# Decay gates of two batches built in one chain and applied on half-height tiles, and a first FFN tile that turns wide

## The chip, the cores and the metric

The kernel runs on one core of a Trainium2 chip. The core has TensorE (PE in the profile, with its weight loads shown apart as PEld), VectorE (DVE), ScalarE (ACT), GpSimd (POOL) and SyncE (SP, which here only issues DMA transfers). The metric is the device time of one execution in microseconds (us), lower is better; a kernel is run several times and the median is given. The profile is one further execution.

## The reference

Causal attention with a forgetting decay over 8 batches of 8 heads, 576 positions, head dimension 64, then a SwiGLU block on the 4608 tokens:

```python
scores = (q @ k.T) / sqrt(64)
cum    = cumsum(log(clip(f, 1e-4, 1)))           # per batch and head
scores = where(causal, -1e9, scores + cum[:, None] - cum[None, :])
attn   = softmax(scores);  x = attn @ v           # x: 4608 tokens x 512
g      = x @ w_gate                               # 512 x 1536
out    = (g * sigmoid(g) * (x @ w_val)) @ w_out   # 1536 x 512
```

## The kernel before

**Order of the work.** The program builds a list of operations, each with an engine (or a choice of engines), a cost, its predecessors, its buffers and a key, and a planner (class `Plan`, L34) plays them through once: at each moment the ready operation with the lowest key goes next on its engine. The order that comes out is fixed for each engine, and every engine works through its own list in order; at run time it waits where a predecessor is late. So a cost, a key or a `ready` time changes only the order. DMA transfers are played in the plan as rings of SP, ACT and POOL that share the bandwidth by `packet`.

**Stages.** Batch 0 is loaded as q and k "quads" by POOL's DMA (`ld_quad`, L472), turned on TensorE (`turn_two`, L477) and copied ("straightened") by ACT or DVE into `QK` (L485, copies at L303 and L305). Its scores come from `score2` (L629): for head pair jj (heads jj and jj+4, on partitions 0 to 63 and 64 to 127) and bank i (a set of key-tile and query-range segments, `BANKS`, L188) first the q.k products of both heads, 64 rows each (L641), then the gate products that add the decay. `expo` (L656, ACT) takes the exponential, `mask` (L660, POOL) blanks the upper triangle, `weigh` (L671, PE) multiplies by V, `invert` and `scale` (DVE) normalise, `flip` (PE) turns the result and `put` copies it to `xT`. Batch 0 goes in two parts: bank 0 of all four pairs, keys from 0 on, then banks 1 to 3 of the four pairs, keys from 1000 on (`attention2`, L749). Batch 1 is turned the same way (`turn`, `straighten`, key S1_KEY = 1150), but its gates, and those of all later batches, are four extra rows of `QK` that SP loads from the DRAM tensor `dec_d` (`rows`, L521), so that `score` (L618) needs one product of 68 rows. Batches 2 to 7 come through DRAM and a transposing DMA (`narrow`, `turned`), from the planned time PACE0 = 61 on.

**Gates of batch 0** (`gates`, L378). The 32 rows of f of batches 0 to 3 are loaded four times, into the four quarters of the partitions. Then, in two parts of 256 and 320 columns: clip (DVE, L324), Ln (ACT, L327), running sum (DVE, L331); from the sum, in bf16, `hi` (-8 cum, its first quarter apart as `hi0`), `mid` and `low` rests (DVE, L342 to L352), and `up` (8 cum, ACT, L336). `KG` holds the key side of the 32 rows over all 128 partitions, `QG` the query side. For a head the right rows are picked by a column of zeros and ones, `chosen` or `three`, which are summed from the identity (L434 to L436): for bank 0 the product takes that column itself, broadcast (L652), and one more product with a column of the identity brings the query side (L653); for banks 1 to 3 DVE has made a copy of `QG` per head with other rows zeroed (`choose`, L372, eight copies of 320 columns) and one product is enough (L650). All of these use 128 rows.

**Gates of later batches.** The 32 rows of batches 4 to 7 (`lf1`) are clipped on DVE early and go through scan, `later` (L360) and four stores on SP from the planned time 36 on, with the low priority key 9000 (DEC1_KEY). `out0` are the four stores of batches 0 to 3.

**FFN.** The tokens go in tiles of 512; per tile 12 column blocks fc: four products with w_gate and four with w_val (L826), tanh on ACT (L830), two DVE operations (L834, L837), then the output products (L841). The first 512 tokens are two tiles of 256, interleaved by block (`share`), and fill PE's gaps in the early stage. The weights come through POOL's DMA in three and four pieces (`weights`, L816). While PE has nothing in the plan, products on the identity run (L930).

The line that is repeated for every segment of a gate product, for bank 0 and for the others:

```python
nc.tensor.matmul(s[:m, c : c + w], keys, row, start=False, stop=end)                       # L650
nc.tensor.matmul(s[:m, c : c + w], keys, three[:, h : h + 1].to_broadcast([P, w]), ...)    # L652
nc.tensor.matmul(s[:m, c : c + w], ident[:, GR + h : GR + h + 1].to_broadcast([P, m]), QG[:, q0 : q0 + w], ...)  # L653
```

Of the kernel before, what the change touches and what calls it, by code (L numbers as in the profile page):

```python
# [9 lines left out]
F32 = mybir.dt.float32  # L10
# [13 lines left out]
class Op:  # L24
    def __init__(self, eng, fn, after, behind, take, use, key, ready, dma):
# [5 lines left out]
        self.start = self.done = None  # L31


class Plan:  # L34
# [32 lines left out]
    def run(self, idle=None):  # L67
# [30 lines left out]
        while left:  # L98
# [4 lines left out]
            while events and events[0][0] <= t + 1e-9:  # L103
                _, _, kind, o = heapq.heappop(events)
                if kind in ("queue", "dma"):
# [10 lines left out]
                    if kind == "queue":  # L116
                        rings[o.ran].append([o.dma, o])
# [82 lines left out]
PACE = 8.8  # L200
PACE_A = 8.8
PACE0 = 61.0
# [4 lines left out]
def kernel(ctx, tc, q, k, v, f, w_gate, w_val, w_out, out):  # L207
# [46 lines left out]
    three = sb("three", [P, H], BF16)  # L254
    chosen = sb("chosen", [P, H], F32)
# [9 lines left out]
    lf1, cum1, rest = [QK[:GR, i, w, : 2 * S].bitcast(F32) for i, w in ((7, 0), (7, 1), (6, 0))]  # L265
    late = [QK[:GR, i, w, n * S : (n + 1) * S] for i, w, n in ((6, 1, 0), (6, 1, 1), (7, 0, 0), (7, 0, 1))]
    ones = OT[0].bitcast(BF16)[:BH, :S]
    KG, QG = xT[:, 0, S : 2 * S], xT[:, 1, S : 2 * S]
    REST = S - HALF
    G0 = {h: xT[:, 3, 2 * S + HALF * n : 2 * S + HALF * (n + 1)] for n, h in enumerate(h for h in range(H) if h % 4 not in ONEHOT)}  # L270
    G1 = [xT[:, n // 3, 2 * S + REST * (n % 3) : 2 * S + REST * (n % 3 + 1)] for n in range(H)]
# [47 lines left out]
    def ld_f(e, half, n):  # L319
        E[e].dma_start(out=lf1 if half else lf[GR * n : GR * (n + 1)],  # L320
                       in_=f.rearrange("b h s -> (b h) s")[GR * half : GR * (half + 1)])

    def clip(e, lf, c):
        E[e].tensor_scalar(out=lf[:, c], in0=lf[:, c], scalar1=1e-4, scalar2=1.0, op0=ALU.max, op1=ALU.min)  # L324
# [10 lines left out]
    def up(e, c):  # L335
        nc.scalar.activation(QG[GR : 2 * GR, c], cum[GR : 2 * GR, c], AF.Copy, scale=8.0)  # L336

    def hi(e, r, c):
        if e == "ACT":
            nc.scalar.activation(KG[r, c], cum[r, c], AF.Copy, scale=-8.0)  # L340
        else:
            nc.vector.tensor_scalar_mul(KG[r, c], cum[r, c], -8.0)  # L342

    def rest1(e, c):
        nc.vector.scalar_tensor_tensor(
            out=r1[64:, c], in0=cum[64:, c], scalar=-8.0, in1=KG[64:, c], op0=ALU.mult, op1=ALU.subtract)

    def mid(e, c):
        nc.vector.tensor_copy(KG[64:, c], r1[64:, c])

    def low(e, c):
        nc.vector.tensor_sub(KG[96:, c], r1[96:, c], KG[96:, c])  # L352

    def dec_out(e, half, n):
        g = slice(GR * half, GR * (half + 1))
        dst = dec_dram[0, 0, g] if n == 0 else dec_dram[n, 1, g]
        src = late[n] if half else QG[GR : 2 * GR] if n == 0 else KG[(0, 64, 96)[n - 1] :][:GR]
        nc.sync.dma_start(out=dst, in_=src)
# [13 lines left out]
    def choose(e, h, part):  # L372
        if part:
            nc.vector.tensor_scalar_mul(G1[h], QG[:, HALF:], chosen[:, h : h + 1])
        else:
            nc.vector.tensor_scalar_mul(G0[h], QG[:, :HALF], chosen[:, h : h + 1])

    def gates(parts, key):  # L378

        lds = [op(("ACT" if n % 2 else "SP", 0.5), ld_f, 0, n, key=-40, dma=0.3, packet=100) for n in range(4)]  # L380
        ld1 = op(("SP", 0.5), ld_f, 1, 0, key=-39, dma=0.3, packet=100)
        done, s = [], None
        lns = []
        for i, c in enumerate(parts):
            w = c.stop - c.start
            a = op(("DVE", 0.1 + w / 960), clip, lf, c, after=lds, key=key - 1 + 0.1 * i, tag="clip")
            lns.append(op(("ACT", 0.15 + w / 1100), ln, lf, c, after=[a], key=key + 0.1 * i, tag="ln"))
# [465 lines left out]
    def ffn(t, t0, n, hs, lo, share):  # L853
# [3 lines left out]
        for fc in range(KF):  # L857
# [5 lines left out]
            if fc == KF - 1:  # L863
                lg = a
# [131 lines left out]
```

## Time and profile before

| | |
|---|---|
| median of 3 runs | 388.75 us (388.27 to 389.16) |
| profiled execution | 388.2 us, its span 386.5 us |
| PE busy in the first 10.4 us | 6.33 us, most of it products on the identity |
| first score product | starts at 10.43 us |
| gate products L650, L652, L653 | 40, 16 and 16 |
| straightens of batch 1, 64x640 and 64x512 | 8 on ACT (771 and 732 ns), 8 on DVE (816 and 716 ns) |
| POOL transfers, issue to landing | quads 9.2 us, V 8.8 us, w_gate and w_val 12.2 us (medians) |

The span is the time from the first to the last instruction. An engine counts as busy while an instruction is in it; products are pipelined and their ends are modelled, so a PE shown as fully busy is not always at its peak, and the distance from the start of one product to the start of the next says more. The chain of waits follows the work that ended last back from its end: at each step to what released it, or to the instruction before it on its engine; asked for a stretch, it starts at the end of that stretch.

### The profile page before, as it was taken

What the parts mean: (1) busy time and instruction counts of PE and PEld (TensorE: products, weight loads), DVE (VectorE), ACT (ScalarE), POOL (GpSimd) and SP (SyncE); (2) the same over time, 40 slices, a digit from 0 to 9 for tenths busy, and PEclk for the clock granted to TensorE, in tenths of its full rate; (3) what the DMA queues carried; (4) which work ended last, traced back from release to release, by engine and by line L of the source; (5) the groups of instructions that cost most, each with busy time, mean ns of one, the idle gap of its engine ahead of it and who ended that gap; (6) DMA issues with size and microseconds to landing.
All of it is one profiled execution on the core that took longest, in us unless ns stands there. A gap on an engine that the chain in (4) does not pass through costs nothing.

```text
span 386.5 us, 8511 instructions
## 1 busy us (share of the span) xinstructions
PE 375.8 (97%) x3185; PEld 216.1 (56%) x3185; DVE 219.5 (57%) x460; ACT 213.8 (55%) x440; POOL 140.1 (36%) x368
## 2 busy tenths in 40 slices
PE   6997999999999999999999999999999999999996
PEld 4666789545556555555555555555564444444444
DVE  8957988257624773277515772477427725733750
ACT  5978884246756565755666457566673323323322
POOL 8794658005534624444355236522330000000000
PEclk9999999999999999999999999999999999999999
DMA  8999998769679994999699999995131011002003
GB/s 165 194 193 195 206 194 133 170 168 171 124 171 204 154 194 94 210 223 180 128 182 199 197 138 213 231 151 85 46 90 46 0 54 57 0 28 83 0 2 109
DMA packets 125065, 52.01 MB, mean 135 GB/s; under 512 B 111840, under 2 KB 119392, under 8 KB 124256
## 3 DMA queue, kind: packets, MB, share of 16 engines
q1 hardware_dynamic: 108640, 36.18, 46.9%
q0 software_dynamic: 16288, 15.14, 26.9%
q8 instruction: 25, 0.41, 0.4%
q10 hardware_dynamic: 96, 0.15, 0.1%
q14 instruction: 16, 0.13, 0.1%
HBM read 38.63 MB, written 17.11 MB: 144 GB/s over the span
## 4 chain that ended last, share of the span: by engine, by line
PE 94%; DVE 2%; ACT 2%; issue 1%; POOL 0%; DVEq 0%; POOLq 0%
PE ps L826 47%; PE ps L841 24%; PE ps L623 9%; PE ps L681 7%; PE ps L650 2%; ACT QK L303 1%; PE ps L641 1%; PE ps L930 1%; PE ps L698 1%; DVE QK L305 1%; PE ps L652 0%; DVE hh L837 0%; PE ps L482 0%; PE ps L498 0%; PE ps L653 0%
## 5 line engine op out<-in xcount | busy, mean ns | idle before, releaser
L826 PE MATMUL ps<-xT,wg 128*128 128x512 bf16 (+1 forms) x480 | 113.0, 357 | 1.1 <-DVE QK L305 1.0
L830 ACT ACTIVATE th<-ps 128x512 f32<-128x512 f32 (+1 forms) x120 | 66.5, 554 | 86.0 <-PE ps L826 83.6
L826 PE MATMUL ps<-xT,wv 128*128 128x512 bf16 (+1 forms) x480 | 113.0, 357 | 0.5 <-DMA wg<-in_moe_w_gate_dram 0.5
L834 DVE SCALAR_TENSOR_TENSOR th<-th,ps 128x512 f32<-128x512 f32 (+1 forms) x120 | 75.6, 630 | 64.9 <-ACT th L830 64.6
L658 ACT ACTIVATE PT<-ps 128x512 bf16<-128x512 f32 (+2 forms) x192 | 92.6, 508 | 27.6 <-PE ps L623 15.8
L841 PE MATMUL ps<-wo,hh 128*128 128x512 bf16 (+2 forms) x456 | 104.5, 367 | 0.0
L837 DVE TENSOR_TENSOR hh<-th,ps 128x512 bf16<-128x512 f32 (+1 forms) x120 | 76.0, 634 | 13.6 <-PE ps L826 1.8
L667 POOL TENSOR_SCALAR_AFFINE_SELECT PT<-PT 128x128 bf16<-128x128 bf16 (+1 forms) x192 | 52.9, 282 | 71.9 <-ACT PT L658 67.2
L826 PEld LDWEIGHTS <-wg 128*128 128x128 bf16 x480 | 45.5, 97 | 41.2 <-issue 1.4
L826 PEld LDWEIGHTS <-wv 128*128 128x128 bf16 x480 | 45.4, 97 | 37.5 <-issue 0.4
L623 PE MATMUL ps<-QK 68*128 68x256 bf16 x392 | 64.8, 261 | 0.0
L841 PEld LDWEIGHTS <-hh 128*128 128x128 bf16 x456 | 41.8, 97 | 37.1
L667 POOL TENSOR_SCALAR_AFFINE_SELECT PTa<-PTa 128x256 bf16<-128x256 bf16 x64 | 26.2, 412 | 76.1 <-ACT PTa L658 74.9
L688 DVE RECIPROCAL rc<-ps 128x5 f32<-128x5 f32 (+2 forms) x68 | 12.9, 190 | 65.5 <-PE ps L681 65.1
L681 PE MATMUL ps<-VB,PT 128*128 128x65 bf16 x768 | 44.2, 193 | 0.8 <-ACT QK L303 0.8
L681 PEld LDWEIGHTS <-PT 128*128 128x128 bf16 x768 | 37.0, 97 | 13.0 <-issue 1.0
L845 ACT ACTIVATE ot<-ps 128x512 f32<-128x512 f32 (+2 forms) x38 | 21.9, 575 | 39.9 <-PE ps L841 38.2
L623 PEld LDWEIGHTS <-QK 68*128 68x128 bf16 x392 | 31.1, 97 | 13.7
L658 ACT ACTIVATE PTa<-ps 128x384 bf16<-128x384 f32 x64 | 30.9, 488 | 10.3 <-PE ps L623 9.5
L693 DVE TENSOR_TENSOR xn<-ps,rc 128x320 bf16<-128x320 f32 (+2 forms) x72 | 32.3, 453 | 2.2
L681 PEld LDWEIGHTS <-PTa 128*128 128x128 bf16 x192 | 13.7, 98 | 11.3
L305 POOL CAST VB<-natv 128x512 bf16<-128x512 f32 (+1 forms) x32 | 19.0, 613 | 0.2 <-DMA natv<-in_v_dram 0.2
(69 smaller groups left out, 158.6 us busy)
## 6 DMA issues: line engine op xcount, KB each, us to landing
out_dram<-ot SPq DMA_DIRECT2D x35, 256.0 KB
natv<-in_v_dram SPq DMA_DIRECT2D x25, 256.0 KB
qk_d<-in_q_dram POOLq DMA_DIRECT2D x24, 144.0 KB, 3.6
qk_d<-in_k_dram POOLq DMA_DIRECT2D x24, 144.0 KB, 4.3
wg<-in_moe_w_gate_dram POOLq DMA_DIRECT2D x3, 512.0 KB, 11.1
wv<-in_moe_w_val_dram POOLq DMA_DIRECT2D x3, 512.0 KB, 12.4
wo<-in_moe_w_out_dram POOLq DMA_DIRECT2D x4, 384.0 KB, 11.9
xT<-in_q_dram POOLq DMA_DIRECT2D x4, 288.0 KB, 8.7
```

The lines of the kernel that those rows point to most:

```text
L305: E[e].tensor_copy(dst, src)
L623: nc.tensor.matmul(s[:, c : c + w], QK[:KR, hqk[p].i, 1, j * S + kt * P : j * S + (kt + 1) * P], QK[:KR, hqk[p].i, 0, j * S + q0 : j * S + ...
L658: nc.scalar.activation(place(h, i)[:, OFFS[i] : OFFS[i] + c], ps(bs)[:, :c], AF.Exp, scale=0.125)
L667: nc.gpsimd.affine_select(out=d, in_=d, pattern=pat, compare_op=ALU.is_ge, fill=0.0, base=0, channel_multiplier=-1,)
L681: nc.tensor.matmul(o[:, lo : lo + D + 1], pt[:, c : c + P], VB[hvb[b].i][:, kt, hb, : D + 1], start=first and n == 0, stop=last and n == l ...
L693: nc.vector.tensor_mul(XN[bx.i][:, qb : qb + nq, j], o, r)
L826: nc.tensor.matmul(ps(bf)[:, :n], w[:, ko, fc * P : (fc + 1) * P], xT[:, ko, t0 : t0 + n], start=(ko == 0), stop=(ko == KD - 1))
L830: nc.scalar.activation(TH[bt.i][:, :n], ps(bf)[:, :n], AF.Tanh, scale=0.5)
L834: nc.vector.scalar_tensor_tensor(out=t, in0=t, scalar=1.0, in1=ps(bf)[:, :n], op0=ALU.add, op1=ALU.mult)
L837: nc.vector.tensor_mul(HH[bh.i][:, lo : lo + n], TH[bt.i][:, :n], ps(bf)[:, :n])
L841: nc.tensor.matmul(ps(bf)[:m, c], HH[hs[fc].i][:, lo : lo + m], wo[:, fc, c], start=(fc == 0), stop=(fc == KF - 1))
L845: nc.scalar.activation(OT[bo.i][:m, c], ps(bf)[:m, c], AF.Copy, scale=0.5)
```

## The change

- **One gate chain for batches 0 and 1.** 16 rows of f (batches 0 and 1) are loaded four times into partitions 0 to 63, and the clip writes them to both halves (two clips per part). The chain runs on all 128 partitions: `hi`, `less`, `mid`, `less`, `low`, where columns of coefficients (`ct`, made of the identity by reductions) let each group of 16 rows end as its own term. `KG` then holds, in each half, four groups of the 16 rows of batches 0 and 1; 64 further columns are set to zero, so that all key tiles are 128 wide.
- **Gate products on 64 rows.** In `score2` the products of heads jj and jj+4 use the rows of their own half, into two banks, as the q.k products do. For banks 1 to 3 there is one copy `QG[jj]` for both heads (four copies of 320 columns, on ACT or DVE); for bank 0 a column `one` and a column of the identity, and `QS` (8 cum).
- **Later gates.** `lf1` now holds all 64 rows; its clip goes to POOL, its scan and `later` get key 1000 and the planned time 12, its stores (48 rows, batches 2 to 7) the planned time 46. `out0` stores the 8 rows of batch 1. `put` of batch 1 no longer comes after the later stores.
- **Exp table.** The first use of Exp (`o_warm`) comes after the three Ln instead of after the first `up`.
- **FFN.** The first tile is one tile of 512 tokens; its blocks 0 to 3 are done in halves of 256, its blocks 4 to 11 whole.
- **Plan.** S1_KEY 1150 becomes 1350 (batch 1's turns come after batch 0's last scores), PACE0 61 becomes 59, costs of some transfers change, and transfers of SP and ACT that enter after 3.5 us while POOL's ring holds small packets are planned 2.5 us later, once.

```diff
-                        rings[o.ran].append([o.dma, o])
+                        if o.ran != "POOL" and t > 3.5 and not o.late and any(r[1].packet < 900 for r in rings["POOL"]):
+                            o.late = True
+                            push(t + LATE, "queue", o)
+                        else:
+                            rings[o.ran].append([o.dma, o])
...
+    KG = xT[:, 3, S : 2 * S]
+    QG = [xT[:, r, n : n + S] for r, n in ((0, S), (1, S), (2, S), (3, 2 * S + D))]
+    KG_ALL = xT[:, 3, S : 2 * S + D]
+    QS = xT[:, 3, 3 * S + D : 3 * S + D + HALF]
...
+    def less(e, n, c):
+
+        nc.vector.scalar_tensor_tensor(out=r1[:, c], in0=KG[:, c], scalar=ct[:, 4 + n : 5 + n], in1=r1[:, c] if n else cum[:, c],
+                                       op0=ALU.mult, op1=ALU.add)
+
+    def mid(e, c):
+        nc.vector.tensor_scalar_mul(KG[:, c], r1[:, c], -8.0)
+
+    def low(e, c):
+        nc.vector.tensor_scalar(out=KG[:, c], in0=r1[:, c], scalar1=ct[:, 7:8], scalar2=ct[:, 8:9], op0=ALU.mult, op1=ALU.add)
...
+            a = [op(("DVE", 0.1 + w / 960), clip, lf[r], c, lf[:D], after=lds, key=key - 1 + 0.1 * i + 0.01 * n, tag="clip")
+                 for n, r in enumerate((slice(D, P), slice(0, D)))]
+            lns.append(op(("ACT", 0.15 + w / 1100), ln, lf, c, after=a, key=key + 0.1 * i, tag="ln"))
...
+            a = op(("DVE", 0.05 + w * 0.0011), hi, c, after=[s], key=kk, tag="hi")
+            a = op(("DVE", 0.05 + w * 0.0015), less, 0, c, after=[a, o_ct], key=kk)
+            a = op(("DVE", 0.05 + w * 0.0011), mid, c, after=[a], key=kk)
+            a = op(("DVE", 0.05 + w * 0.0015), less, 1, c, after=[a], key=kk)
+            a = op(("DVE", 0.05 + w * 0.0011), low, c, after=[a], key=kk, tag="low")
+            u = op(("ACT", 0.15 + w / 1100), up, c, after=[s], key=kk, tag="up") if i == 0 and ONEHOT else None
...
+        l1 = op(("ACT", 0.67), ln, lf1, slice(0, S), after=[a], key=key + 0.3, tag="ln1")
+        a = op(("DVE", 1.4), scan, cum1, lf1, slice(0, S), after=[l1], key=DEC1_KEY, ready=DEC1_AT, tag="scan1")
...
+    o_warm = op(("ACT", 1.4), lambda e: nc.scalar.activation(warm, warm, AF.Exp), after=lns, key=WARM_KEY)
...
-                keys = KG[:, kt * P : kt * P + m]
+                r, end = slice(D * u, D * (u + 1)), n == len(segs) - 1
+                o, keys = ps(bs[u])[:, c : c + w], KG_ALL[r, kt * P : (kt + 1) * P]
                 if i or jj not in ONEHOT:
-                    row = G1[h][:, q0 - HALF : q0 - HALF + w] if i else G0[h][:, q0 : q0 + w]
-                    nc.tensor.matmul(s[:m, c : c + w], keys, row, start=False, stop=end)
+                    nc.tensor.matmul(o, keys, QG[jj][r, q0 : q0 + w], start=False, stop=end)
                 else:
-                    nc.tensor.matmul(s[:m, c : c + w], keys, three[:, h : h + 1].to_broadcast([P, w]), start=False, stop=False)
-                    nc.tensor.matmul(s[:m, c : c + w], ident[:, GR + h : GR + h + 1].to_broadcast([P, m]),
-                                     QG[:, q0 : q0 + w], start=False, stop=end)
+                    mine = D * u + 6 * H + FB * u + jj
+                    nc.tensor.matmul(o, keys, one[r, jj : jj + 1].to_broadcast([D, w]), start=False, stop=False)
+                    nc.tensor.matmul(o, ident[r, mine : mine + 1].to_broadcast([D, P]), QS[r, q0 : q0 + w], start=False, stop=end)
...
+            parts = [(0, HALF), (HALF, n - HALF)] if t == 0 and fc < WIDE else [(0, n)]
...
-S1_KEY = 1150
+S1_KEY = 1350
-CLIP1 = ('DVE', 0.43)
+CLIP1 = ('POOL', 2.1)
-DEC1_KEY = 9000
-DEC1_AT = 36
+DEC1_KEY = 1000
+DEC1_AT = 12
+DECOUT_AT = 46
+WIDE = 4
```

203 lines of the change are left out of this document (91 added, 112 removed).

## The prediction

> **What bounds the kernel now.** I read the busy times by stage first, then the chain of waits of three early stretches, then the groups of single lines. The whole span first: time, engine, then busy microseconds.
>
> ```profile
> span 386.5 us, 8511 instructions
> PE 375.8 (97%) x3185; PEld 216.1 (56%) x3185; DVE 219.5 (57%) x460; ACT 213.8 (55%) x440; POOL 140.1 (36%) x368
> ```
>
> PE is the bound of the whole, so the end moves only by PE work that disappears or by PE gaps that close. The stages say where gaps are (stretch, its length, then busy us and count of each engine, clock, DMA share, GB/s):
>
> ```profile
> 10.40:14.00 3.60, 3.55 (x100) 2.77 (x100) 3.40 (x10) 3.15 (x7) 2.39 (x5) 1.00 2.25 161
> 14.00:30.00 16.00, 16.00 (x238) 10.90 (x235) 10.39 (x39) 13.08 (x30) 14.59 (x37) 1.00 1.38 198
> 30.00:38.00 8.00, 5.33 (x95) 4.47 (x96) 5.84 (x12) 7.24 (x14) 3.12 (x7) 1.00 1.44 197
> 38.00:50.00 12.00, 11.55 (x117) 9.57 (x117) 11.06 (x27) 10.47 (x27) 8.94 (x21) 1.00 1.21 204
> 50.00:68.00 18.00, 18.00 (x241) 16.11 (x240) 15.32 (x44) 11.35 (x29) 11.76 (x30) 1.00 0.95 162
> ```
>
> From 50 on PE has no gap until the last store; 30 to 38 has 2.67 us of gaps, 38 to 50 has 0.45. Everything that the change touches lies before 68, so the question is how much PE time it takes out of 10.4 to 50. The chain of 10 to 18 shows what PE does there (start, us, what):
>
> ```profile
> 14.89 0.27 PE ps L641 x4
> 15.16 0.21 PE ps L652
> 15.38 0.11 PE ps L653
> 15.49 0.11 PE ps L652
> 15.60 0.11 PE ps L653
> ...
> 16.97 0.27 PE ps L641 x4
> 17.24 0.56 PE ps L650 x4
> 17.79 0.18 PE ps L681 x6
> ```
>
> The reader sees q.k products (L641, 64 rows each) and gate products (L650, L652, L653, 128 rows each). The four L641 stream 256, 256, 128 and 128 columns. At the pace of L652/L653 (a new 256-column product every 0.11 us) they would take 0.32 us one after another, but the next begins after 0.27: the two heads, on different halves of the rows, run side by side, 0.16, and then there is a gap of 0.11. The gates are not side by side: one per 0.11. In 30 to 38 the chain is another:
>
> ```profile
> 30.72 0.78 ACT QK L303
> 32.42 0.83 DVE QK L305
> 33.27 0.78 ACT QK L303
> 35.70 0.77 ACT QK L303
> 36.49 0.74 ACT QK L303
> 37.26 0.73 DVE QK L305
> ...
> 41.85 1.27 DVE QK L331
> 43.15 0.56 DVE QK L364
> 44.56 0.66 DVE QK L366
> ```
>
> There the copies of batch 1's turned q and k on ACT and DVE, and then the late gate chain on DVE, end the waits.
>
> **The change, part by part.** The sum is made against the profiled execution, 388.2 us (span 386.5 and 1.7 around it); the median of the runs shown is 388.75, so 0.55 is added at the end.
>
> Gate products. For each of four head pairs, bank 0 now has eight 128-row products (four of 256, four of 128 columns: 4 x 0.107 + 4 x 0.053 = 0.64 us); they become eight 64-row ones, two at a time: 0.32. Banks 1, 2 and 3 have 2 x (192+320), 2 x (64+320) and 2 x 320 columns at 0.417 ns: 0.43, 0.32, 0.27; halved, 0.51 saved. Per pair 0.83, in all **-3.3**. If the pairs did not overlap it would be 0, if they overlap as L641 does it is all of it; I take all, since L641 is the same shape on the same rows.
>
> Gaps between the two shapes. After each of the 16 L641 groups 0.11 us pass before the gate products; with both on 64 rows this may vanish: 0 to -1.7. I take half, **-0.8**, as a gap is still due wherever a 128-row product (L681) comes next. The Trainium skill ("TensorEngine Tiling (Array Packing)", Key Properties) states that a change of tiling mode drains TensorE. By that rule all 1.7 would go and the sum would be 0.9 lower; the trace's gap of 0.11 agrees with a drain, but which neighbours remain is not shown, so the sum keeps half.
>
> Start. Before the first score at 10.43 the chain holds the Exp table load (8.35, 1.28 us) and its first use (0.20) between two straightens on ACT. The key side was turned by 9.07 (L482), so at best the score comes 0.7 earlier once the load is moved ahead. Against that: the load now waits for all three Ln, the last of them for a clip on POOL; DVE loses the two memsets (0.60) and the sums L434 to L436 (0.45), gains about ten small ones of 0.12 to 0.17 (1.2 to 1.7) behind the identity, two more clips of about 0.3 to 0.4, and a chain of 5 instead of 4 (256 columns: 0.29+0.42+0.29+0.42+0.29 = 1.71 against 1.42). The memsets left before 4.4 cover about 1 us of it. Range -0.7 to +1.0, I take **-0.2**.
>
> POOL's clip. The 576-column clip leaves DVE (0.91, L324) and goes to POOL behind the fourth quad load, at 4.9. No row shows it on POOL: the cast of 512 columns takes 0.613 (0.69 at 576), the 256-column mask 0.41, which at 576 and twice for two operations is 1.85. I take 1.85, the masks being nearer to an ALU operation. Queued behind it on POOL are five loads of V (0.84 each), two weight loads, and then the masks. POOL had 1.2 us idle before the first mask at 12.02 and 0.8 at 15.1, so most is covered; without that cover it is 1.85 on the first mask. Behind ACT's Ln for it stand the table load and straightens. **+0.3**, range 0 to 1.85.
>
> DVE and ACT. Gone: eight picks (8 x 0.419 = 3.4 on DVE), `up` and `hi0` of the second part and `hi0` of the first (0.47+0.47+0.42 on ACT). New: four picks on DVE or ACT (0.32 to 0.47). Moved: the late chain (1.34+0.56+0.74+0.50+0.74 = 3.9 on DVE, 0.67 on ACT) from 41.8 to somewhere after 12. DVE has 5.6 us idle in 14 to 30, which hides it; where it stood, PE had only 0.42 us of waits: **-0.4**, range 0 to -0.5. Its four stores stay at about 46 on SP, with batch 2's V loads behind them as before (49.24). The loads of f shrink from five of 72 KB to four of half and one of double that; the four stores of batch 1's rows stay.
>
> First FFN tile. Of 12 column blocks, 8 go from two halves to one: 128 products of 256 columns (0.110 each, 14.1 us) become 64 of 512 (0.216, 13.8): **-0.3**. ACT saves 8 x (2 x 0.38 - 0.55), DVE 16 x (2 x 0.41 - 0.63), about 1.7 and 3.0 us, both under a PE without gaps from 50 on: 0. Wide blocks need all 512 tokens of batch 0; four narrow ones (4 x 1.76 = 7 us of PE) stand ahead of them, and the turns of batch 1 now come after the scores, so the second half is ready sooner. Batch 2's release, planned 2 us earlier (59 for 61), falls where PE has no gap: 0.
>
> What comes back. PE saves 4.1 us inside 10.4 to 30, but ACT is busy 16.2 of 19.6 there; with -0.94 for the second `up` and `hi0`, +0.94 for half the picks and +0.67, its slack is 2.7. ACT waits for PE in that stretch for some 2.4 us (1.5 on L650, 0.6 on L653, 0.3 on flips). Only that can close, so 1.7 must come back as new PE gaps, all 4.1 if nothing closes. FFN blocks could fill a part, but each 256-wide one costs ACT 0.38 and DVE 0.83. I take **+2.0**, range 0 (later gaps fill) to 4.1.
>
> Sum: -3.3 - 0.8 - 0.2 + 0.3 - 0.4 - 0.3 + 2.0 = -2.7: 385.5 for the profiled execution, **386.0** as a median. Own range of this case 384.3 to 387.6. A difference of 0.2%, 0.8 us, is about what a measurement tells here.
>
> **Rivals.** *ACT and DVE take it all back*: the stretch to 38 is theirs already (7.24 of 8 us on ACT, copies in the chain), PE only waits longer. For it: these rows, and ACT's total early work hardly changes. Against: in 14 to 30 the chain is PE alone. Price: 4.1 come back instead of 2.0: 388.1. The Trainium skill ("TensorEngine Tiling (Array Packing)", PSUM Bottleneck) says just this: tiling speeds TensorE, not the emptying of PSUM. The trace bears it out in 30 to 38, not in 14 to 30.
>
> *Everything counts*: the saved time stays, the drain gaps go, and the 2.67 us of gaps in 30 to 38 are filled, since copies of batch 1 come when FFN work is at hand. Without the 2.0 and with 0.9 more of gaps: -5.6, 383.1. Against it: the copies still need 12 us of ACT and DVE.
>
> *Slower: POOL's queue sets the first 50 us.* POOL is busy 13.4 of 14 us in 16 to 30, and everything loaded by it is moved by the clip's 1.85. If landing, not PE, ends the waits (first weigh on V, copies on the quads, FFN on weights), the PE saving is idle time and the delay is paid: +1.85 - 0.3 and 0.5 for ACT's Ln in order: +2.1, 390.8. It decides as soon as the queue's delay exceeds its backlog. For it: L474 waited 0.8 on a V load, L826 0.5 on a weight load. Against: loads land 9 to 12 us after issue, so issue is ahead of transfer.
>
> *The pairs do not overlap*: no 3.3, no gaps saved, nothing to come back: -0.6, 388.15. L641 speaks against it.
>
> **How the numbers follow.** Forecast 0.47; everything counts 0.15; taken back 0.12; no overlap 0.04; POOL's queue 0.22. Faster: the first two and a little of the next, 0.64; same 0.14; slower 0.22. The range goes from 383.0 (the best case) to 390.8 (POOL's case), leaving out the outer halves of these, 0.18.
>
> **What would show it.** Gate products of two heads in pairs 0.11 us apart for 256 columns: the first step. No 0.11 gap after L641: the second. First score before 10.4 and the table load before the first straighten: the start. ACT above 90% in 14 to 30 with PE gaps that ACT ends: what comes back. POOL idle before its first mask: the clip covered; a first weigh that waits for DMA, or PE gaps above 4 us in 10 to 40, would make the prediction wrong, and so would batch 0's last weigh later than 33.4.

## The result, and the profile after

The changed kernel takes 387.87 us (median of 9 runs, 387.40 to 388.35), the kernel before 389.16 beside it (9 runs, 388.27 to 389.94): 0.9968 of the time before, 95% interval 0.9957 to 0.9979, so 1.24 us less. In two further rounds of runs (chips 9 and 5) the ratio was 0.9960 [0.9946, 0.9973] and 0.9956 [0.9939, 0.9972]. The forecast was 2.75 less (386.0 for 388.75): the direction held, less than half of the size came. The profiled execution took 387.93. The first lines of its page: span, busy time of each engine, and the granted TensorE clock in 40 slices of 9.65 us:

```profile
span 386.2 us, 8313 instructions
...
PE 372.8 (97%) x3082; PEld 208.8 (54%) x3129; DVE 218.3 (57%) x445; ACT 212.9 (55%) x433; POOL 142.6 (37%) x369
...
PEclk9699999999999999999999999999999999999999
```

PE is busy 3.0 us less than before (372.8 for 375.8), but the span is only 0.3 shorter. The second slice of the clock row has a 6. The stages that the prediction showed, now in the changed kernel, in the same columns (stretch, length, then busy us and count of PE, PEld, DVE, ACT, POOL, then clock, DMA share, GB/s):

```profile
10.40:14.00 3.60, 3.08 (x61) 2.43 (x62) 3.46 (x7) 3.08 (x7) 3.60 (x6) 0.52 2.16 166
14.00:30.00 16.00, 15.38 (x256) 9.95 (x256) 12.83 (x39) 13.46 (x32) 15.23 (x33) 0.89 1.46 189
30.00:38.00 8.00, 6.87 (x126) 5.28 (x125) 7.14 (x16) 7.02 (x14) 5.24 (x15) 1.00 1.39 199
38.00:50.00 12.00, 11.66 (x103) 8.76 (x102) 8.02 (x19) 10.50 (x26) 6.39 (x18) 1.00 1.22 196
50.00:68.00 18.00, 17.83 (x192) 11.12 (x193) 13.60 (x28) 11.31 (x24) 10.35 (x29) 1.00 0.86 154
```

PE's gaps from 10.4 to 38 were 2.72 us and are 2.27; the clock, 1.00 there before, is 0.52 in the first stage and 0.89 in the second. In steps of 2 us:

```profile
8.00:10.00 2.00, 1.06 (x40) 0.76 (x39) 1.82 (x8) 1.64 (x4) 1.94 (x3) 1.00 1.20 231
10.00:12.00 2.00, 1.21 (x40) 0.98 (x40) 2.00 (x4) 1.48 (x3) 2.00 (x3) 0.64 1.68 188
12.00:14.00 2.00, 2.00 (x25) 1.45 (x22) 1.86 (x5) 2.00 (x5) 2.00 (x4) 0.50 2.45 154
14.00:16.00 2.00, 2.00 (x42) 1.30 (x41) 1.06 (x3) 0.95 (x3) 1.71 (x3) 0.50 2.04 174
16.00:18.00 2.00, 2.00 (x25) 1.06 (x23) 2.00 (x6) 1.76 (x5) 1.52 (x3) 0.65 1.24 206
```

PE runs at half speed for 1.44 + 2 + 2 + 1.40 = 6.8 us (if the clock is either full or half, 0.64 is half speed for 1.44 of 2 us, and so on), after a stretch in which it was busy only about half of the time. "PE busy 2.00" does not tell half speed from full. The half that is lost is 3.4 us of PE work, in the very stage where the side-by-side products save theirs. The products themselves (the timeline; start, duration):

```profile
17.50 0.34 PE L658 MATMUL ps<-QK 64*128 64x256 bf16 x4
17.68 0.27 PE L669 MATMUL ps<-one,xT 64*128 64x256 bf16 x2
17.79 0.27 PE L670 MATMUL ps<-xT,ident 64*128 64x256 bf16 x2
17.90 0.22 PE L669 MATMUL ps<-one,xT 64*128 64x128 bf16 x2
17.95 0.22 PE L670 MATMUL ps<-xT,ident 64*128 64x128 bf16 x2
```

Each line of L669 and L670 is a pair, one product per head: 0.11 us for two of 256 columns, 0.05 for two of 128, and from the q.k products (L658) to the first gate product 0.18 with 0.16 of columns: no gap of 0.11. The Trainium skill ("TensorEngine Tiling (Array Packing)", Key Properties) says that TensorE drains when the tiling mode changes; the rows agree, since 64 rows follow 64 rows here without the gap.

The start came later. The chain of waits up to the first score product:

```profile
3.50 7.38 DMA xT<-in_q_dram
10.88 0.04 issue
10.93 0.99 PE ps L499 x21
11.91 0.43 PE ps L658 x4
```

The third quad lands at 10.88, its turn (L499) stands ahead of the first score in PE's order, and the first score starts at 11.84 (before 10.43). The quads take 5.4 to 8.1 us from issue to landing, before 4.4 to 7.4: the two stores of ones on SP now start at 2.73 instead of 3.49, beside them. In two further traces of the changed kernel the first score starts at 11.43 and 11.75.

**One measure for all runs.** The first output product (`wo`, L857) starts at 67.75 in the kernel before and at 67.63 after, and from there to the end 318.75 and 318.6 us pass; in 15 of the 18 runs below it is 318.6, in e4, g1 and g3 318.3 to 318.8. So a difference in span is made before that product, and for those 15 its start tells it to about 0.1 us in one traced execution.

### The profile page after: what moved, and what is told of

It is laid out like the page before. It is cut to its first block, busy times and chain, and to the rows that moved or that the text cites. A ratio compares the mean times of both kernels' runs of the same rounds, so it can differ in the third digit from the quotient of the medians.

```text
span 386.2 us, 8313 instructions
## 1 busy us (share of the span) xinstructions
PE 372.8 (97%) x3082; PEld 208.8 (54%) x3129; DVE 218.3 (57%) x445; ACT 212.9 (55%) x433; POOL 142.6 (37%) x369
## 3 DMA queue, kind: packets, MB, share of 16 engines
q0 software_dynamic: 16288, 15.14, 26.1%
## 4 chain that ended last, share of the span: by engine, by line
PE 92%; DVE 2%; DMA 2%; ACT 1%; issue 1%; POOL 1%; ACTq 0%; POOLq 0%
PE ps L842 48%; PE ps L857 24%; PE ps L640 10%; PE ps L697 7%; DMA xT<-in_q_dram 2%; PE ps L658 1%; ACT QK L309 1%; DVE QK L311 1%; PE ps L714 1%; DVE xn L709 1%; PE ps L944 1%; PE ps L499 0%; ACT PT L674 0%; POOL xT L491 0%; PE ps L666 0%
## 5 line engine op out<-in xcount | busy, mean ns | idle before, releaser
L846 ACT ACTIVATE th<-ps 128x512 f32<-128x512 f32 (+1 forms) x112 | 65.3, 583 | 84.2 <-PE ps L842 82.8
L842 PE MATMUL ps<-xT,wg 128*128 128x512 bf16 (+1 forms) x434 | 109.8, 371 | 0.8
L842 PE MATMUL ps<-xT,wv 128*128 128x512 bf16 (+1 forms) x432 | 109.7, 371 | 0.9
L850 DVE SCALAR_TENSOR_TENSOR th<-th,ps 128x512 f32<-128x512 f32 (+1 forms) x112 | 74.6, 666 | 63.2 <-ACT th L846 63.0
L857 PE MATMUL ps<-wo,hh 128*128 128x512 bf16 (+2 forms) x439 | 101.5, 367 | 0.9
L853 DVE TENSOR_TENSOR hh<-th,ps 128x512 bf16<-128x512 f32 (+1 forms) x112 | 74.8, 669 | 12.3 <-PE ps L842 0.8
L842 PEld LDWEIGHTS <-wg 128*128 128x128 bf16 x448 | 42.5, 97 | 41.2 <-issue 0.2
L640 PE MATMUL ps<-QK 68*128 68x256 bf16 x392 | 63.8, 260 | 0.1
L842 PEld LDWEIGHTS <-wv 128*128 128x128 bf16 x448 | 42.2, 97 | 38.7
L857 PEld LDWEIGHTS <-hh 128*128 128x128 bf16 x456 | 42.2, 97 | 37.8
L697 PE MATMUL ps<-VB,PT 128*128 128x65 bf16 x768 | 43.1, 193 | 0.8 <-issue 0.7
L709 DVE TENSOR_TENSOR xn<-ps,rc 128x320 bf16<-128x320 f32 (+2 forms) x72 | 32.3, 453 | 2.2
L697 PEld LDWEIGHTS <-PTa 128*128 128x128 bf16 x192 | 13.7, 98 | 12.6 <-POOL PTa L683 1.1
L311 POOL CAST VB<-natv 128x512 bf16<-128x512 f32 (+1 forms) x32 | 19.1, 616 | 0.0
## 6 DMA issues: line engine op xcount, KB each, us to landing
wg<-in_moe_w_gate_dram POOLq DMA_DIRECT2D x3, 512.0 KB, 10.4
```

The source lines that it names most:

```text
L311: E[e].tensor_copy(dst, src)
L640: nc.tensor.matmul(s[:, c : c + w], QK[:KR, hqk[p].i, 1, j * S + kt * P : j * S + (kt + 1) * P], QK[:KR, hqk[p].i, 0, j * S + q0 : j * S + ...
L697: nc.tensor.matmul(o[:, lo : lo + D + 1], pt[:, c : c + P], VB[hvb[b].i][:, kt, hb, : D + 1], start=first and n == 0, stop=last and n == l ...
L709: nc.vector.tensor_mul(XN[bx.i][:, qb : qb + nq, j], o, r)
L842: nc.tensor.matmul(ps(bf)[:, :n], w[:, ko, fc * P : (fc + 1) * P], xT[:, ko, t0 : t0 + n], start=(ko == 0), stop=(ko == KD - 1))
L846: nc.scalar.activation(TH[bt.i][:, :n], ps(bf)[:, :n], AF.Tanh, scale=0.5)
```

## The experiments

"Ratio" is against the kernel before on the same chip; "first output" is the start of the first output product in the traced execution, "clock" the mean granted clock of that execution.

| kernel | median us | ratio, 95% interval | span | first score | first output | clock |
|---|---|---|---|---|---|---|
| before | 389.16 | 1 | 386.5 | 10.43 | 67.75 | 0.999 |
| changed | 387.87 | 0.9968 [0.9957, 0.9979] | 386.2 | 11.84 | 67.63 | 0.991 |
| r_after | 387.62 | 0.9960 [0.9946, 0.9973] | 385.7 | 11.43 | 67.09 | 0.996 |
| k1_after | 387.32 | 0.9956 [0.9939, 0.9972] | 385.6 | 11.75 | 67.02 | 0.996 |
| e1_dummies | 387.15 | 0.9966 [0.9952, 0.9980] | 385.3 | 11.52 | 66.67 | 1.000 |
| f2_full | 389.59 | 1.0004 [0.9988, 1.0021] | 388.3 | 11.72 | 69.67 | 0.991 |
| f2d_full_dum | 387.91 | 0.9974 [0.9962, 0.9986] | 385.7 | 11.43 | 67.11 | 1.000 |
| f1_dum_late | 386.40 | 0.9938 [0.9921, 0.9956] | 386.5 | 13.78 | 67.88 | 1.000 |
| k2_late | 387.07 | 0.9953 [0.9937, 0.9969] | 384.8 | 11.41 | 66.22 | 1.000 |
| e2_ones_late | 386.79 | 0.9949 [0.9931, 0.9968] | 385.7 | 11.43 | 67.09 | 0.996 |
| g2_noclip1 | 386.94 | 0.9956 [0.9939, 0.9972] | 385.0 | 11.27 | 66.36 | 1.000 |
| h4_late_ones_dum | 386.41 | 0.9918 [0.9897, 0.9939] | 384.7 | 11.41 | 66.09 | 1.000 |

The traced execution of f1 was its slowest of six (388.19); the other five took 386.35 to 386.59. The low ratio of h4 owes something to the kernel before, which ran 389.73 on that chip; by medians f1 and h4 are alike.

**Are the products side by side because of their order?** e3 issues all gate products of one head, then those of the other:

```diff
-        for n, (kt, q0, w, c) in enumerate(segs):
-            for u in range(2):
+        for u in range(2):
+            for n, (kt, q0, w, c) in enumerate(segs):
```

> The changed kernel with the gate products of a bank issued head after head instead of alternating, so that they can't run side by side; same products, same order otherwise. If the side-by-side products are worth what the prediction took for them, 3.3 us: the time rises by 2 to 4 us, the more since part of them runs at half clock. If the early stage is bound by ACT and DVE: less than 1 us.

387.47 us, 0.9964 [0.9952, 0.9976]: no price, for they still run in pairs. Its timeline has the same starts 0.11 and 0.05 apart, though the four products of one head now stand ahead of those of the other:

```profile
17.37 0.34 PE L658 MATMUL ps<-QK 64*128 64x256 bf16 x4
17.55 0.29 PE L669 MATMUL ps<-one,xT 64*128 64x256 bf16 x2
17.66 0.29 PE L670 MATMUL ps<-xT,ident 64*128 64x256 bf16 x2
17.77 0.23 PE L669 MATMUL ps<-one,xT 64*128 64x128 bf16 x2
```

So the run did not measure what the pairs are worth. f2 did: the gate products again on all 128 rows (each head's scores then get the gate terms of both heads of its pair, so the output is not the reference's; the count and the columns of the products stay).

```diff
-                nc.tensor.matmul(o, keys, QG[jj][r, q0 : q0 + w], start=False, stop=end)
+                nc.tensor.matmul(o, keys, QG[jj][:, q0 : q0 + w], start=False, stop=end)
...
-                keys = KG_ALL[r, kt * P : (kt + 1) * P]
+                keys = KG_ALL[:, kt * P : (kt + 1) * P]
```

(and the same for L669 and L670). f2d has the filler of e1 besides.

> The changed kernel with its gate products over all 128 rows again (one head after the other; each head then gets the sum of both heads' gates, so the output is another). Issued head after head they still ran side by side, so this is the run that prices it. If the side-by-side products are worth the 3.3 us of the prediction's first step and PE bounds the stretch: 3 to 6 us above the changed kernel (more than 3.3 since part runs at half clock). If waits on DVE, ACT and transfers bound it: less than 1 us.

> The same, and the three identity products in slots 14 to 20 that hold the clock at 1.0. If DVE bounds 14 to 22 us once the clock is held: at most 0.7 us above the variant with the identity products alone. If PE bounds it: 2.5 to 3.5 above.

> The changed kernel itself, to stand beside the variants on the same chip. All theories: 0.4 to 1.5 us below the kernel before.

f2 took 389.59 (1.0004), f2d 387.91 (0.9974), the changed kernel on the same chip 387.62 (0.9960). Without the row halves the change is no gain at all, unless the filler is there. f2 lies 1.97 above the changed kernel, between its two expectations (3 to 6, less than 1); f2d lies 0.76 above e1 by medians and 0.3 by ratio, which is the side of DVE and not the 2.5 to 3.5 of PE.

**Does the half clock cost?** e1 holds the clock: where the order has one filler product on the identity in slots 14 to 20 of its list, it has three.

```diff
+        slots[0] += 1
+        for _ in range(3 if 14 <= slots[0] <= 20 else 1):
             nc.tensor.matmul(z[:, :HALF], ident, ident.unsqueeze(1).to_broadcast([P, 2, P]), start=True, stop=True)
```

> The changed kernel, with three identity products instead of one in the slots 14 to 20 (between the turns, where PE waits for the q and k quads). Clock theory: the granted clock stays at 1.0 between 10 and 17 us (it was 0.64, 0.50, 0.50, 0.65), the scores there go at their full pace and the time falls by 1.5 to 3 us, to about 385.5. Rival (ACT and DVE take everything back in the early stage): the clock recovers, the time stays within 0.5 us of 387.9.

e1 took 387.15 (0.9966). The clock came back, but the time did not fall by 1.5 to 3 us: it is 0.7 lower by medians and not lower by ratio. e1 and f2d belong together with the two kernels without filler. First output product in one traced execution each, not all on one chip:

| | clock 0.991 | clock held |
|---|---|---|
| gate products on 128 rows | 69.67 (f2_full) | 67.11 (f2d_full_dum) |
| on 64 rows | 67.63 (changed) | 66.67 (e1_dummies) |

With the clock held, side by side is worth 0.44 us (0.3 by the ratios of the medians, 0.9974 and 0.9966); with a half clock 2.04 (1.7 by 1.0004 and 0.9960). The half clock costs 2.6 with 128 rows, 0.96 with 64. The runs of f2, which has no filler, say the same by themselves: 387.43 and 387.44 at a clock of 1.000, four of 389.14 to 389.25 at 0.994 or 0.995, three of 389.99 to 390.03 at 0.991. (Three more of 389.93 to 390.08 show 1.000; they are open, like five of the changed kernel below.) The filler holds the clock: PE busy 1.90 and 1.86 of 2 us in 8 to 10 and 10 to 12 in e1, clock 1.00 all through, and at 0.995 or above in all 36 runs of e1, f2d, f1 and h4, above 0.998 in 35 of them. Yet e1's ratio of medians (0.9966) is not below that of the changed kernel; f1 below shows what stands there next. Nor are the runs alike at full clock: e1 goes from 386.57 to 388.99 (the slowest at 1.000), f2d from 387.41 to 389.67 (at 0.999). What moves them is open.

k1 is the changed kernel once more, on one chip with k2 (which has the late gate chain back at its old key and time, 9000 and 36):

```diff
-DEC1_KEY = 1000
-DEC1_AT = 12
+DEC1_KEY = 9000
+DEC1_AT = 36
```

> The changed kernel itself, on one chip with k2_late, so that the late chain is priced by the two alone: 387.5 to 388.0, clock near 0.99 in most runs.

> The late gate chain back at key 9000 and 36 us, beside the changed kernel on one chip. If its place at 17 us costs what identity products with and without it showed: 0.6 to 0.8 us below k1_after. If it costs only what its DVE time took from the normalisations in the trace of the changed kernel (0.60 of waits): 0.3 to 0.6 below. If it shows only where the clock is held: within 0.2.

k1 took 387.32, k2 387.07 (0.9953 [0.9937, 0.9969]): 0.25 less, inside the spread of both, and too little for either theory of a cost (0.3 to 0.6, 0.6 to 0.8). Their windows of the first stage differ all the same, k1 first:

```profile
10.00:12.00 2.00, 1.17 (x40) 1.14 (x42) 2.00 (x4) 1.58 (x3) 2.00 (x3) 0.67 1.75 185
12.00:14.00 2.00, 2.00 (x26) 1.43 (x23) 1.86 (x5) 2.00 (x5) 2.00 (x4) 0.50 2.46 154
14.00:16.00 2.00, 2.00 (x53) 1.27 (x51) 1.68 (x4) 1.35 (x4) 1.74 (x4) 0.98 1.89 177
```

k2:

```profile
10.00:12.00 2.00, 1.18 (x50) 1.11 (x52) 2.00 (x4) 1.80 (x4) 2.00 (x3) 1.00 1.51 188
12.00:14.00 2.00, 2.00 (x58) 1.38 (x53) 1.86 (x5) 2.00 (x5) 2.00 (x4) 1.00 2.40 160
```

PE was equally idle ahead of it in both (1.09 of 2 us from 8 to 10), and the clock fell in one and not in the other. In k1 the spell of half speed is 1.32 + 2 + 0.08 = 3.4 us, in the changed kernel's first trace 6.8, in r_after's (0.91, 0.50, 0.74) 3.4. The 22 runs of the changed kernel sort by it only in part: 386.52 and 386.99 at 1.000; seven of 387.30 to 387.44 at 0.996; most of 387.81 to 388.35 at 0.990 to 0.998; but five of 387.81 to 387.85 show 1.000. What those five lost is open. The kernel before never fell below 0.998 in 91 runs.

The clock of each run allows a comparison of like with like (us; the traced executions with 0.991 had a spell of 6.8 us, those with 0.996 one of 3.4):

| kernel | at 0.990 or 0.991 | at 0.996 | best at 0.999 or 1.000 |
|---|---|---|---|
| changed, 22 runs | 387.87 to 388.10 | seven of nine 387.30 to 387.44 | 386.52 |
| e2_ones_late | 387.83 | 387.40 | 386.50 |
| g2_noclip1 | 388.03 | 387.22 | 386.64 |
| e5_narrow | 388.09, 388.24 | 387.43 to 387.65 | 386.70 |
| k2_late, and h1_late with the same edit | 387.90 to 388.06 | 386.80 to 386.89 | 386.53 |

So the late chain costs the changed kernel 0.5 us at 0.996 and nothing that shows at 0.990 or in the best runs; three further runs of k2 at 0.999 or 1.000 took 387.26 to 387.73, so its time too moves at full clock. e2, g2 and e5 are taken up below.

**The late chain.** h1 is the same edit as k2 on another chip, f1 has it with e1's filler.

> The variant with three identity products, and the late gate chain back at key 9000 and planned time 36. DVE theory (scan and rests of the late chain, 3.9 us, stand among the normalisations of batch 0's first part and hold the flips that PE waits for): PE's gaps in 18 to 24 close and the time falls 0.7 to 1.5 us below that variant. Rival (DVE is as full at 41 to 49, so the chain costs the same there): within 0.4 us of it.

> Only the late gate chain is put back to key 9000 and planned time 36; nothing else differs from the changed kernel (0.9968 and 0.9960 of before). Theory A, the late chain among the normalisations costs PE time, and in the identity-product version its removal gave 0.9938 against 0.9966: ratio 0.994 to 0.9955, no L377 before 35 us, and the first normalisations wait for PE alone. Rival B, the gain came from both edits together (the chain only shows where the clock is held): 0.996 to 0.997, and the granted clock again near 0.5 in 12 to 16 us. A ratio of 0.998 or more would mean that the stage after 36 pays the chain as it did before.

f1 386.40, against 387.15 of e1 on another chip: 0.75 less by medians (0.6 by the commonest values, 386.4 and 387.0), at the lower end of the DVE theory. h1 0.9944 [0.9921, 0.9966]; the kernel before ran 389.73 on that chip, so k1 and k2 decide for the pair without filler. The trace of e1 shows why the chain costs where the clock is held:

```profile
18.13 1.87 DVE L377 TENSOR_SCALAR QK<-QK 64x576 bf16<-64x576 f32 x1
...
18.20 1.49 POOL L683 TENSOR_SCALAR_AFFINE_SELECT PTa<-PTa 128x256 bf16<-128x256 bf16 x4
...
20.91 0.49 DVE L709 TENSOR_TENSOR xn<-ps,rc 128x128 bf16<-128x128 f32 x2
...
21.26 0.29 PE L714 MATMUL ps<-ident,xn 128*128 128x128 bf16 x2 [1.61 <-DVE xn L709]
```

The chain's first rest (L377, 0.56 in the kernel before, 1.10 in the changed one) takes 1.87 beside POOL's masks, the next normalisations (L709) stand behind it, and PE waits 1.61. With the chain at 36 the gap is gone (PE busy 3.99 of 4 us in 18 to 22 in k2, 3.88 in f1, e1 2.39), and with the gates on 128 rows it is not there either (f2d 3.93). In the first trace of the changed kernel, with its spell of 6.8 us, PE waits only 0.60 there, in r_after and k1, with 3.4, it waits 1.35 and 1.32: the later the half clock makes PE, the shorter its wait for DVE.

**The start and POOL's clip.** e2 holds the two stores of ones on SP until the first `low` is done (a store cannot leave before a two-column memset behind `low` has written the tile again). g2 leaves out POOL's clip of the f rows of batches 2 to 7; f lies between 0.8 and 1.0, so nothing is cut by it. e4 puts the clip on DVE. g1 loads f into all eight groups of partitions, so that one clip per part is enough; g3 is g1 with the edits of e2 and k2.

```diff
-            nc.sync.dma_start(out=dec_dram[0, 1], in_=ones)
+            held_ones.append(lambda: nc.sync.dma_start(out=dec_dram[0, 1], in_=ones))
...
+        if c.start == 0:
+            nc.vector.memset(ones[:1, :2].bitcast(F32), ONE2)
+            while held_ones:
+                held_ones.pop(0)()
```

```diff
-        src = lf if src is None else src
+        if src is None:
+            return
```

```diff
-CLIP1 = ('POOL', 2.1)
+CLIP1 = ('DVE', 0.7)
```

> The changed kernel, the two stores of ones on SP held until the first part of the gate chain ends (one tiny memset on DVE more). Transfer theory: the four quads land 1.0 to 1.6 us sooner (5.7, 7.4, 9.8, 11.6 us as before the change, instead of 6.7, 9.0, 10.9, 12.3), the first score starts about 1 us sooner, and the time falls by 1 to 2 us. Clock theory alone: the sooner quads also shorten PE's waits, so the clock stays up for longer. Rival (ACT and DVE): quads land sooner and the time stays within 0.5 us.

> The changed kernel with the 576-column clip on POOL left out (the values of f lie between the bounds, so the result is the same); the order of all else stays. If POOL's 2.66 us and the wait before it are paid (V loads at 8.98 instead of 5.9, first mask at 14.5, first weigh at 17.3): the first weigh comes 1 us or more sooner and the time falls by 0.5 to 1.5 us. If they are covered: within 0.3 us of the changed kernel.

> The changed kernel with the 576-column clip on DVE again (planned 0.7 us there; the plan is made anew, so orders shift). If the 2.66 us of POOL and its wait for f are what delays V, the weights and the second quads: those are issued 3 us sooner and the time falls by 1 to 2 us. If loads are ahead of need anyway: within 0.5 us of 387.9.

> The changed kernel with f loaded into all eight groups of 16 rows, so that one clip per part on all rows replaces the two per part on half of them; the plan is made anew. Start theory (the longer DVE chain ahead of the key-side straighten, 4.5 to 10.8 us without a gap, holds the first score at 11.8): the gate chain ends some 0.9 us sooner, the first score starts near 11.0 and the time falls by 0.5 to 1 us below the changed kernel. Rival (the start is covered, only 18 to 40 counts): within 0.3 us.

> The changed kernel with f in eight groups, the stores of ones held as before, and the late chain back at key 9000 and time 36. If start, quads and late chain each cost what the single runs suggest (0.5 to 1, 0.6, 0.6 us): about 1.7 us below the changed kernel, 386.0 or less, the fastest so far. If they hide each other: no better than the best single one, 386.4.

e2 386.79, 0.9949 [0.9931, 0.9968]; g2 386.94, 0.9956 [0.9939, 0.9972], with the first score at 11.27 and the first weigh product at 15.14 (changed 17.27). By ratio their medians are 0.3 to 0.7 (e2) and 0 to 0.5 (g2) below the three sets of the changed kernel, but the best runs are not: 386.50 and 386.64, against 386.52. At the same clock both are within 0.2 of it (the table above), and the traced executions of e2 and r_after, both at 0.996, have the same first score (11.43) and the same first output product (67.09). In e2 the last three quads do land 1.4 us sooner, but the third turn then waits 1.4 us for a copy on DVE (L311), as it does in k1 (1.33). So what e2 and g2 give is not handed on by itself; the rows allow that it works through the clock (four of six runs of each are at 0.999 or above, against 7 of 22, of which five are the unexplained ones), and six runs do not settle that. How long the clip is, and what two operations on DVE take, the groups of the changed kernel show (line, shapes, count, busy us, mean ns, idle before):

```profile
L333 POOL TENSOR_SCALAR QK<-QK 64x576 f32<-64x576 f32 x1 | 2.7, 2657 | 0.4 <-DMA QK<-in_f_dram 0.4
```

```profile
L345 DVE TENSOR_SCALAR xT<-xT 128x256 bf16<-128x256 f32 x1 | 0.6, 574 | 0.0
...
L454 DVE CAST one<-ct 128x4 bf16<-128x4 f32 x1 | 0.4, 384 | 0.0
```

and those of g2, the same two operations with no clip on POOL:

```profile
L346 DVE TENSOR_SCALAR xT<-xT 128x256 bf16<-128x256 f32 x1 | 0.3, 294 | 0.0
...
L455 DVE CAST one<-ct 128x4 bf16<-128x4 f32 x1 | 0.2, 171 | 0.0
```

The 2.66 us are not the clip's work alone: in 13 traces it starts between 6.22 and 6.72 and ends at 8.90 to 8.93 all the same, and where it starts later it takes 2.17 or 2.18 (h1, g1, g3). L345 runs beside it, but an operation of the same form that follows (L353, from 8.12) takes its 0.29 beside it too. The cast starts at 9.51, after the clip has ended at 8.92, and takes 0.36 in e4 as well, so its 0.38 is not the clip's doing.

e4 was slower, 389.37 and 1.0008 [0.9993, 1.0023], but its order changed with the clip's engine (68 FFN weight loads before 50 us for 77), so it says nothing of the clip alone. The same holds for g1, 391.73 and 1.0072 [1.0059, 1.0085], and g3, 390.65 and 1.0042 [1.0028, 1.0057]: the first score came at 10.44 and 10.14, but the new order put the Ln of the later rows between two exponentials, and ACT loaded tables three times:

```profile
12.74 1.28 ACT L673 ACT_TABLE_LOAD   x1
14.04 0.49 ACT L673 ACTIVATE PTa<-ps 128x384 bf16<-128x384 f32 x1
14.54 1.28 ACT L336 ACT_TABLE_LOAD   x1
15.84 0.68 ACT L336 ACTIVATE QK<-QK 64x576 f32<-64x576 f32 x1
16.54 1.28 ACT L468 ACT_TABLE_LOAD   x1
```

h3 has the late chain back and no clip:

> Late chain back at 36 us and POOL's clip of the rows of batches 2 to 7 left out (the values of f lie in 0.8 to 1.0, so the result stays). Theory A, POOL's clip costs by itself (first mask, first weigh, the quads' neighbours on DVE): 0.3 to 0.5 us below the late chain alone, 0.993 to 0.994. Rival B, the clip cost only because the late chain was slowed beside POOL's later masks: equal to the late chain alone within 0.15 us.

387.09, 0.9930 [0.9908, 0.9953], beside h1 (387.52) 0.43 less, its rival being 0.15 at most: by medians the clip costs 0.4 when the late chain is out of its way, while g2 shows next to nothing at the same clock. Six runs each, 0.4 apart, do not settle it.

**The first FFN tile.** e5 does all twelve blocks in halves (`WIDE = 12`).

> The changed kernel with all 12 column blocks of the first FFN tile in halves (as before the change). Prediction's term: the wide blocks are worth 0.3 us on PE, so this is 0.3 us slower. If the relief of ACT and DVE (1.7 and 3.0 us) or the later start of wide blocks counts too: 0.5 to 1.5 us slower, or faster.

387.65, 0.9970 [0.9959, 0.9982]; its first output product starts at 67.24, against 67.02 and 67.09 of the two executions of the changed kernel at the same clock, 0.996: the wide blocks are worth some 0.2. The medians do not resolve that; at the same clock e5 is 0.1 to 0.2 slower.

**Together.** h2 has the late chain back and the stores held, h4 two filler products for one in slots 14 to 20 besides.

> Late chain back at 36 us and the two stores of ones on SP held behind the first `low`. The two cost -0.7 us and -0.5 us when taken out one at a time. If they are separate terms: 0.992 to 0.9935. If the third turn's wait for a DVE copy (1.41 us with the stores held) eats it: no better than the late chain alone.

> Late chain back, stores held, and two identity products in place of one in slots 14 to 20. If the half clock of 10.7 to 17.3 us is what is left, 0.991 to 0.9925 and a granted clock of 1.0 from 10 us on; if DVE and the copies set the early stage, 0.993 or above, with the wait of PE's weight load on DVE ahead of the first score longer than 1 us.

h2 386.81, 0.9929 [0.9907, 0.9951]; h4 386.41, 0.9918 [0.9897, 0.9939], all six runs between 386.40 and 386.48. That is 1.46 less than the first nine runs of the changed kernel and 0.9 less than k1, though on another chip; the single runs of the changed kernel reach 386.52 at best. With the late chain back, the filler makes nearly every run like the best (all of h4, five of six of f1); with the chain early it does not (e1, f2d). The held stores add nothing to that: f1 does without them, at 386.40.

## Why the prediction was right in direction and wrong in size

**Balance.** In traced executions, with the start of the first output product as the measure: before 67.75; all of the change but the 64 rows, clock held, 67.11 (f2d): -0.64, where the prediction's other terms (-0.2, +0.3, -0.4, -0.3) had come to -0.6, an agreement that is luck, since the start and the late chain had the wrong sign; the 64 rows, 66.67 (e1): -0.44; the half clock, 67.63: +0.96. In sum -0.12, and 0.15 behind that product (318.75 to 318.6): -0.3 of span. The medians fell by more, 1.24, because the traced execution of the kernel before was close to its best (388.2, where the nine runs took 388.27 to 389.94), while that of the changed kernel was at its median. The prediction added the same 0.55 to both; for the changed kernel it was -0.06. The direction was luck in part: the change brought the half clock itself, and by f2 (1.0004) it would have gained nothing without the row halves, which are worth 2.04 there for the 0.44 that they are worth at full clock.

**Gate products -3.3 and gaps -0.8: right as sizes on PE.** Pairs start 0.11 apart, and the gap behind the q.k products is gone. From start to start, all q.k and gate products of batch 0 take 12.6 us in the kernel before and 8.3 and 8.5 in k2 and e1, at full clock: 4.1 to 4.3 less.

**What comes back +2.0: the step that failed first.** Of the 4.1 that PE saves (3.2 between f2d and e1, whose q.k and gate products take 11.7 and 8.5), 0.44 stays with the clock held, so 2.8 to 3.7 come back, near the upper end of 4.1 and near the rival "ACT and DVE take it all back", whose 388.1 is close to the 387.87 measured. The prediction took ACT's slack of 2.7 us as the measure. It was DVE that ended most of the new waits: PE is idle for 1.23 us from 10 us to the first output product in f2d and for 3.36 in e1, and of the 2.1 more DVE ended 1.9, 1.61 of them the normalisations behind the late chain. With the chain back at 36 some 0.6 of the 3.7 are regained (f1); where the rest goes, which shows in no long gap, was not taken apart. The rule that the prediction weighed, that tiling speeds TensorE and not the emptying of PSUM (the Trainium skill, "TensorEngine Tiling (Array Packing)", PSUM Bottleneck), came nearer than the forecast; but the operation that PE waited for, though it empties PSUM (L709), was late for the chain ahead of it.

**The clock: a step that was missing.** The sum counted PE work at the clock of the kernel before, 1.00 in every stage that it showed. The changed start leaves PE busy 1.06 and 1.21 of 2 us in 8 to 12, and the clock fell to half for 3.4 or 6.8 us in most runs: 0.96 in the traced execution, some 0.4 with the shorter spell (67.02 and 67.09 for 66.67). The signs that were to make the prediction wrong were gaps, above 4 us from 10 to 40; in the first trace there were fewer than before (2.8 for 3.2), since a slow PE counts as a busy one, in r_after and k1 4.0 and 3.7. One sign did come, a last weigh of batch 0 later than 33.4: the last of its 120 products starts at 37.3. But it starts at 36.4 in the kernel before, so the sign was set too early.

**Start -0.2: wrong sign.** The first score came 1.0 to 1.4 later in three traces, at or outside the end of the range, +1.0. DVE's four clips took 1.84 us where two had taken 0.72, two small operations took 0.57 and 0.38 for 0.29 and 0.17, the stores of ones pushed the quads back, and the third turn stands ahead of the first score. By itself it cost the end little: g2 starts at 11.27 and ends no earlier in its best runs. That it cost something by leaving PE idle ahead of the half clock is likely, and not shown.

**POOL's clip +0.3: not settled, and each part was off.** Leaving it out gives 0.4 by medians in h3 and next to nothing at the same clock in g2. It lasted 2.17 to 2.71 us instead of 1.85, and the first mask came at 14.54 for 12.02. The rival "POOL's queue sets the first 50 us" did not come: the first mask was 2.5 us late and the first weigh product 2.7 (17.27 for 14.55), and that was not paid at the end.

**Late chain -0.4, hidden by DVE's idle time: wrong.** 0.25 us is won by putting it back in the kernel as it is (not resolved; 0.5 among the runs at 0.996), 0.6 to 0.75 where the clock is held. Idle time over 16 us was no cover, since the chain stood in order ahead of normalisations that PE waited for.

**First FFN tile -0.3**: about 0.2. **Pairs do not overlap**: refuted by the starts 0.11 apart. **Everything counts**: refuted; the early saving was given back before 50 us.

**The table load** did not go before the first straighten: it waited for POOL's clip by way of the last Ln and ran from 9.65 to 10.93.

## What to carry to other kernels

A saving on a busy engine in a starting stage is worth what the next engine leaves of it: here 0.44 of 4.1 us, and some 0.6 more when the operations that stand in order ahead of the next engine's urgent ones were moved away. Read the granted clock beside each busy time, in windows of 2 us, and fill the waits of an opening stage with cheap products if the clock falls there; here that paid once DVE's chain was out of the way. Idle time summed over a stage is no cover for an operation that has a fixed place in an in-order queue.

## What the runs showed of the hardware that was not expected

- The clock falls for spells of 3.4 or 6.8 us after PE was busy for 2.3 to 2.8 of the 4 us from 8 to 12, and not in every run of the same program: 386.52 to 388.35 us. k2's trace, with 2.27 of 4, kept the full clock, and so did e1's behind 18 to 22, with 2.39 of 4; e4, whose trace has 3.75 of 4 in 8 to 12, shows 0.991 to 0.996 in four of 12 runs, where in them is not on record. So the share alone does not decide, and no run shows what does. The Trainium skill ("TensorE: Matmul & The Clock Gate", What's actually happening) gives a free-running window of some 3.4 us after which the clock is set anew, so that the outcome varies from run to run; the lengths of the spells, 3.4 and twice 3.4, agree. It speaks of an idle window; here a half-busy one was often enough.
- Products on the two halves of the rows run side by side whichever order they are issued in, over at least four products of one half (e3).
- POOL's two-operation clip of 64x576 in fp32 lasts 2.17 to 2.71 us, and its end is the same for starts 0.5 us apart; DVE took 0.91 for 32x576 in the kernel before.
- A DVE operation and POOL's masks hold each other up for whole operations. In eight traces L377 begins beside a run of three or five masks and ends 0.31 or 0.32 us after the last of them, whatever its length comes to (1.09 to 1.88). In the others it goes ahead of the next mask and takes 0.44 to 0.69, and that mask ends 0.26 or 0.27 us after it (0.10 in g3). So the 1.87 is mostly waiting, and masks that follow each other closely let it in only at their end. The Trainium skill ("SBUF — State Buffer", Who interferes with whom) says that some one-input DVE operations block with POOL's for whole instructions; the lengths agree, and no run tells which form of L377 does it.
